# Fetching the experts' weights and tokens one step ahead, and issuing sinkhorn's steps in smaller pieces

## The chip, the cores and the metric

The kernel runs on one core of one Trainium2 chip. A core has TensorE (PE, with its weight loads as PEld), VectorE (DVE), ScalarE (ACT), GpSimd (POOL) and SyncE (SP), which here only issues DMAs. Each engine works through its own instructions in the order in which they were issued. The metric is the device time of one execution in microseconds, as the median of several runs.

## The reference, cut to what matters

```python
# 1. delta-rule attention, 768 steps for 4 x 8 heads; its output is x, 3072 x 384
# 2. a dense layer: h = x @ w_in (384 x 2048); x = (h * tanh(softplus(h))) @ w_out
# 3. eight experts, mixed by a doubly normalised gate
logits = x @ w_gate                       # 3072 x 8
P = np.exp(logits - logits.max())
for _ in range(8):
    P /= P.sum(1, keepdims=True) + 1e-09
    P /= P.sum(0, keepdims=True) + 1e-09
    P *= N / E
for e in range(E):
    h = np.maximum(x @ w1[e], 0.0)        # 384 x 1024
    out += P[:, e:e + 1] * (h @ w2[e])    # 1024 x 384
```

## The kernel before

The tokens are cut into six blocks of 512 (NBLK). The **first part** goes through the blocks one by one: attention, the dense layer in 16 steps (s0 to s15, with f1 to f4 behind them), and expert 0 in 8 steps (s16 to s23). Every step uses one weight tile `w` of 768 KB out of six slots; `conversions` asks for the next tile at the end of a step (L242, `w<-wd`). Each block's x goes to DRAM as `x2d`, expert 0's sum as `y0d`.

The **second part** does experts 1 to 7 in 168 *pairs* `(e, i, g)`: expert, block, and one of four groups of 256 hidden columns; g runs fastest, then i. For pair p, `first(p)` (L470) makes the seven sums of a fast block-matrix scheme (33 matmuls) in four PSUM banks b0 to b3. Two of them come from pool `ps_h`, two from `ps_a`; both pools have two buffers. `evacuate(p)` adds them up on DVE (L493 to L496), with a copy and a relu on ACT (L492, L497), and splits the result into a high and a low part `gh`, `gl` (L498). `second(p)` (L1329) multiplies them by w2 into the banks `o`. PE's order is first(p), second(p-1), first(p+1) and so on.

Around this the following is issued in program order, so that each piece stands in a place of its own on each engine:

- `g_load` brings one group's weights: two DMAs into the one raw tile `gr` (L401, L405, issued by `g_fetch` within g_load), four additions on DVE (L421 to L424), two copies on ACT (L426), four subtractions on POOL (L428). Five slots (`gslots`) hold results; two of them lie in memory that comes free only when the first part is over. Loads 0 to 2 stand at s1, s5 and s9 of the last block, loads 3 and 4 ahead of first(0), the others behind the second products of an expert's last block.
- `x_begin(i)` fetches a block's tokens into the one raw tile `gxr` (L436) and makes four sums on DVE (L438 to L441); `x_split` splits them in three portions on ACT and POOL (L448, L449); `x_store` writes the result to DRAM as `xcd` (2304 KB), from where later experts read it by `x_load` (L457). In expert 1 block i+1 is begun at g = 0, split at g = 1 to 3 and stored at g = 3, where `acc_load(i + 2)` also fetches an accumulator from `y0d` (L1350).
- The sinkhorn normalisation is a list `sinks`, of which `sink_step` takes one. `sink_start` has two small products on PE, `sink_round` is DVE alone (L349 to L353), `sink_round_end` begins with a product on PE of what the round left (L357, 8 columns, in a `ps_a` buffer) and goes on on DVE (L359 to L362). Two steps are taken per step s17 to s23 of the last block, then two per pair.
- When the list is empty, each pair scales two quarters of an accumulator by expert 0's gate on DVE (L1390).

Of the kernel before, what the change touches and what calls it, by code (L numbers as in the profile page):

```python
# [28 lines left out]
U1 = DFF // 128  # L29
# [55 lines left out]
def delta_mish_sinkhorn_kernel(  # L85
# [245 lines left out]

    def sink_start():
        m1, m2, m3 = sk["m"][:, 0:1], sk["m"][0:1, 1:2], sk["m"][:, 2:3]
        nc.vector.tensor_reduce(out=m1, in_=Pf, axis=AX.X, op=ALU.max)
        ps = small[0]()
        nc.tensor.transpose(ps[0:1, 0:128], m1, id_sb)
        nc.vector.tensor_reduce(out=m2, in_=ps[0:1, 0:128], axis=AX.X, op=ALU.max, negate=True)
        ps2 = small[0]()[:, 0:1]
        mm(ps2, lhsT=sk["ones"][0:1, :], rhs=m2, start=True, stop=True)
        nc.vector.tensor_copy(m3, ps2)  # L340
        nc.scalar.activation(out=Pf, in_=Pf, func=AF.Sigmoid, bias=m3)
        d = sk["d"]
        nc.vector.tensor_scalar(out=d, in0=Pf, scalar1=-1.0, scalar2=1.0, op0=ALU.mult, op1=ALU.add)
        nc.vector.reciprocal(out=d, in_=d)
        nc.vector.tensor_tensor(out=Pf, in0=Pf, in1=d, op=ALU.mult)
# [18 lines left out]
    sinks = deque([sink_start, lambda: None] + [sink_round, sink_round_end] * ROUNDS)  # L364
# [32 lines left out]
    def g_fetch(n):  # L397
# [11 lines left out]
        return r  # L409

    def g_load():
# [6 lines left out]
        r = g_fetch(n)  # L418
# [6 lines left out]
        for at in (1024, 0):  # L425
            nc.scalar.activation(out=w[:, 0, at:at + 1024], in_=r[:, at:at + 1024], func=AF.Copy)  # L426
            for q in (at, at + 512):
                nc.gpsimd.tensor_tensor(  # L428
                    out=w[:, 1, q:q + 512], in0=r[:, q:q + 512], in1=w[:, 0, q:q + 512].bitcast(F32), op=ALU.subtract
                )  # L430

    def x_begin(i):

        c = order[i]
        r = pool2["xr"].tile([128, NX, 256], F32, tag="xr", name="gxr")
        nc.sync.dma_start(out=r[:, 0:6].rearrange("p a x -> p (a x)"), in_=x2_dram[c].rearrange("p k x -> p (k x)"))  # L436
# [5 lines left out]
        xraw[i] = r  # L442
# [67 lines left out]
    if True:  # L510
# [708 lines left out]
        with tc.manual_schedule():  # L1219
            banks[:] = [0, [A1, A1]]  # L1220
            for c in range(NBLK):
                pe, rest, late = window(c)
                if c == NBLK - 1:
                    p1.close()
                    open_second()
                    for f, step in ((1, g_load), (5, g_load), (9, g_load)):
                        rest[f"s{f}"].append(step)
                    rest["s12"].append(lambda: x_begin(0))
                    for k in range(3):
                        rest[f"s{13 + k}"].append(lambda k=k: x_split(0, k))  # L1230
                    rest["f1"].append(lambda: x_store(0))
# [49 lines left out]
                for f in range(U1, NU):  # L1281
# [9 lines left out]
                    if c == NBLK - 1 and f > U1:  # L1291
                        sink_step()
                    if f > U1 + 1:
                        y0_second(u - 2)
                    if c == NBLK - 1 and f > U1:
                        sink_step()
# [46 lines left out]
    with tc.manual_schedule():  # L1343
# [12 lines left out]
        while gnext[0] < NGS:  # L1356
            g_load()
        for p in range(N + 1):
# [6 lines left out]
            if p >= 1:  # L1365
                second(p - 1)
                if pairs[p - 1][1] == NBLK - 1:
                    g_load()
            if p < N:
                if e == 1:  # L1370
                    if i + 1 < NBLK:
                        if g == 0:
                            x_begin(i + 1)
                        elif g < NGR - 1:
                            x_split(i + 1, g - 1)
                        else:
                            x_split(i + 1, 2)
                            x_store(i + 1)
                            acc_load(i + 2)
                    elif g == NGR - 1:  # L1380
                        x_load(p + 1)
                elif g == 1 and p + NGR < N:
                    x_load(p - 1 + NGR)
# [70 lines left out]
```

## Time and profile before

| | |
|---|---|
| median of 3 runs | 2407.23 us (2403.13 to 2412.72) |
| the profiled execution, its own time | 2409.84 us |
| its span, first to last instruction | 2408.1 us |
| mean granted TensorE clock | 0.960 of full speed |
| PE busy | 2260.9 us, 94% |
| PEld, DVE, ACT, POOL busy | 2092.1, 1228.7, 619.7, 529.0 us |

A timeline row gives the start (us from the span's start), the length, the engine, the line, the operation, what it writes and reads, how many instructions were merged, and in square brackets the idle time of its engine just before it with what ended that. An idle time of PE is what the end can move by; an idle time of DVE, ACT or POOL counts only where PE waits for them. The last block's first part begins near 836 us, the second part at 951.20 us.

### The profile page before, as it was taken

What the parts mean: (1) busy time and instruction counts of PE and PEld (TensorE: products, weight loads), DVE (VectorE), ACT (ScalarE), POOL (GpSimd) and SP (SyncE); (2) the same over time, 40 slices, a digit from 0 to 9 for tenths busy, and PEclk for the clock granted to TensorE, in tenths of its full rate; (3) what the DMA queues carried; (4) which work ended last, traced back from release to release, by engine and by line L of the source; (5) the groups of instructions that cost most, each with busy time, mean ns of one, the idle gap of its engine ahead of it and who ended that gap; (6) DMA issues with size and microseconds to landing.
All of it is one profiled execution on the core that took longest, in us unless ns stands there. A gap on an engine that the chain in (4) does not pass through costs nothing.

```text
span 2408.1 us, 41970 instructions
## 1 busy us (share of the span) xinstructions
PE 2260.9 (94%) x18012; PEld 2092.1 (87%) x18012; DVE 1228.7 (51%) x2009; ACT 619.7 (26%) x1012; POOL 529.0 (22%) x439
## 2 busy tenths in 40 slices
PE   6698899999999998598989999999999999999998
PEld 3477788788887877598989999999999999999998
DVE  8874726426171204554545455555555555555554
ACT  4244331333322241212221121122122113112111
POOL 5586441332412060211210030020011003002000
PEclk7799999999999999799989999999999999999999
DMA  5357634536344474133132221222212223212321
GB/s 170 115 203 220 221 133 149 185 132 223 130 169 155 163 246 182 41 117 132 69 142 79 93 88 71 93 93 105 89 56 105 79 93 119 79 72 88 105 78 55
DMA packets 74442, 297.05 MB, mean 123 GB/s; under 512 B 7504, under 2 KB 39504, under 8 KB 68880
## 3 DMA queue, kind: packets, MB, share of 16 engines
q1 hardware_dynamic: 74256, 294.36, 35.3%
q8 instruction: 142, 2.33, 0.4%
q14 instruction: 44, 0.36, 0.0%
HBM read 247.15 MB, written 47.19 MB: 122 GB/s over the span
## 4 chain that ended last, share of the span: by engine, by line
PE 33%; issue 11%; DMA 6%; POOL 3%; SPq 0%; ACT 0%; DVE 0%; POOLq 0%; DVEq 0%; ACTq 0%
PE b L470 17%; PE o L1329 16%; DMA gr<-in_w_dram 5%; POOL gw L428 2%; POOL gx L428 1%; DMA acc<-y0d 1%; DMA gx<-xcd 0%; SPq L401 0%; DVE gt L493 0%; ACT gw L426 0%; POOL gx L449 0%; DVE acc L1334 0%; ACT gh L497 0%; SPq L457 0%; ACT gx L448 0%
## 5 line engine op out<-in xcount | busy, mean ns | idle before, releaser
L470 PE MATMUL b<-gx,gw 128*128 128x256 f32 x3564 | 457.4, 286 | 11.0 <-DVE gt L493 6.3
L470 PEld LDWEIGHTS b<-gx,gw 128*128 128x128 f32 x3564 | 449.4, 195 | 15.5 <-DVE gt L493 7.8
L1329 PE MATMUL o<-gw,gh 128*128 128x384 f32 x1728 | 440.9, 336 | 2.3 <-DVE acc L1334 2.3
L497 ACT ACTIVATE gh<-gt 128x1024 fp32r<-128x1024 f32 x168 | 178.3, 1062 | 657.0 <-DVE gt L496 657.0
L1329 PEld LDWEIGHTS o<-gw,gh 128*128 128x128 f32 x1728 | 307.7, 189 | 3.0 <-issue 2.1
L296 PE MATMUL psh<-xh,w 128*128 128x512 f32 x864 | 290.3, 418 | 19.1 <-DMA w<-wd 6.8
L498 DVE SCALAR_TENSOR_TENSOR gl<-gt,gh 128x1024 fp32r<-128x1024 f32 x168 | 207.3, 1234 | 189.5 <-ACT gh L497 189.5
L1329 PE MATMUL o<-gw,gl 128*128 128x384 f32 x864 | 289.7, 335 | 0.0
L493 DVE TENSOR_TENSOR gt<-b,gt 128x512 f32<-128x512 f32 x168 | 116.1, 691 | 316.5 <-PE b L470 257.1
L470 PE MATMUL b<-gx,gx 128*128 128x256 f32 x1980 | 246.1, 282 | 13.5 <-DMA gx<-xcd 12.5
L470 PEld LDWEIGHTS b<-gx,gx 128*128 128x128 f32 x1980 | 242.7, 190 | 15.2 <-issue 13.2
L1329 PE MATMUL o<-gx,gh 128*128 128x384 f32 x960 | 247.5, 339 | 1.6 <-DVE acc L1334 1.6
L428 POOL TENSOR_TENSOR gw<-gr,gw 128x512 fp32r<-128x512 f32 x72 | 90.7, 1294 | 573.4 <-ACT gw L426 573.4
L296 PEld LDWEIGHTS psh<-xh,w 128*128 128x128 f32 x864 | 161.2, 196 | 60.0 <-issue 12.3
L961 POOL TENSOR_TENSOR gl<-x,gh 128x512 fp32r<-128x512 f32 x96 | 128.6, 1341 | 381.7 <-ACT gh L960 381.5
L296 PE MATMUL psh<-xl,w 128*128 128x512 f32 x432 | 176.2, 408 | 4.2 <-DVE xl L590 4.2
L1329 PEld LDWEIGHTS o<-gx,gh 128*128 128x128 f32 x960 | 171.6, 188 | 1.9 <-issue 1.0
L1329 PEld LDWEIGHTS o<-gw,gl 128*128 128x128 f32 x864 | 162.6, 188 | 0.3 <-DVE gl L498 0.2
L1329 PE MATMUL o<-gx,gl 128*128 128x384 f32 x480 | 162.7, 339 | 0.0
L492 ACT ACTIVATE gt<-b 128x256 f32<-128x256 f32 x168 | 64.2, 382 | 370.6 <-PE b L470 347.9
L972 PE MATMUL x<-gh,w 128*128 128x512 f32 x576 | 149.5, 395 | 0.0
L428 POOL TENSOR_TENSOR gx<-gr,gx 128x512 fp32r<-128x512 f32 x40 | 50.3, 1290 | 430.7 <-ACT gx L426 430.7
(182 smaller groups left out, 2993.0 us busy)
## 6 DMA issues: line engine op xcount, KB each, us to landing
w<-wd SPq DMA_DIRECT2D x120, 768.0 KB, 4.5
gx<-xcd SPq DMA_DIRECT2D x36, 2304.0 KB, 8.9
gr<-in_w_dram SPq DMA_DIRECT2D x56, 384.0 KB, 3.7
wd<-w SPq DMA_DIRECT2D x24, 768.0 KB, 4.6
xcd<-gx SPq DMA_DIRECT2D x6, 2304.0 KB, 7.9
kq<-in_qkb_dram SPq DMA_DIRECT2D x20, 256.0 KB, 7.0
vt<-in_vtok_dram SPq DMA_DIRECT2D x6, 768.0 KB, 8.4
kq<-in_w_in_dram SPq DMA_DIRECT2D x12, 384.0 KB, 4.6
```

What stands on the lines that cost most here:

```text
L296: mm(ps, lhsT=wi(u, pw, kc), rhs=(xh, xl)[px][:, kc, :], start=(n == 0), stop=(n == 3 * KD - 1))
L428: nc.gpsimd.tensor_tensor(out=w[:, 1, q:q + 512], in0=r[:, q:q + 512], in1=w[:, 0, q:q + 512].bitcast(F32), op=ALU.subtract)
L470: mm(ps, lhsT=w[:, pw, a * 128:a * 128 + 128], rhs=x[:, px, b, :], start=(n == 0), stop=(n == last))
L492: nc.scalar.activation(out=t[:, 7], in_=b0[:, 0], func=AF.Copy)
L493: tt(out=t[:, 0:7:6], in0=b1, in1=t[:, 7:8].to_broadcast([128, 2, 256]), op=ALU.add)
L497: nc.scalar.activation(out=h, in_=t[:, 0:4], func=AF.Relu)
L498: nc.vector.scalar_tensor_tensor(out=l, in0=t[:, 0:4], scalar=0.0, in1=h.bitcast(F32), op0=ALU.max, op1=ALU.subtract)
L961: nc.gpsimd.tensor_tensor(out=l, in0=p, in1=h.bitcast(F32), op=ALU.subtract)
L972: mm(x2ps[c][k], lhsT=wo(u, pw, k * 128, k * 128 + 128), rhs=(h, l)[pg], start=(f == 0 and n == 0), stop=(f == U1 - 1 and n == 2))
L1329: mm(o[t], lhsT=(h, l)[ph][:, z, (t % 2) * 128:(t % 2) * 128 + 128], rhs=w[:, pw, at:at + DM], start=(g == 0 and fi == 0 and n == 0), stop ...
```

## The change

- `g_fetch` leaves `g_load` and stands at its end, for the next load. The very first one is issued alone at s1; g_loads 0 to 2 move to s5, s9 and s13.
- `x_fetch` leaves `x_begin`. Block 0 is fetched at s1, block 1 at s15, block i + 2 when block i + 1 has been split, ahead of that block's store and the accumulator. x_begin(0) and its splits move to s7, s8, s10 and s11, its store to s15.
- g_loads 3 and 4 no longer stand ahead of first(0) but behind second(0) and second(4) (`p in (1, 5)`). The following loads stay where they were.
- `x_load` is issued at g = 0 instead of g = 1 (four pairs ahead instead of three); the first one, for expert 2, is issued at pair 20 instead of pair 23.
- `sink_start` is divided into sink_max, sink_max_all and sink_start with empty steps between them. The list has 22 entries instead of 18. In s17 to s23 two steps are taken together, ahead of expert 0's second product. In the pairs two are taken behind evacuate(p) and two more behind second(p-1).

```diff
@@ -329,12 +329,16 @@
     P = lg
     Pf = lg.rearrange("p t e -> p (t e)")
 
+    def sink_max():
+        nc.vector.tensor_reduce(out=sk["m"][:, 0:1], in_=Pf, axis=AX.X, op=ALU.max)
+
+    def sink_max_all():
+        ps = small[0]()
+        nc.tensor.transpose(ps[0:1, 0:128], sk["m"][:, 0:1], id_sb)
+        nc.vector.tensor_reduce(out=sk["m"][0:1, 1:2], in_=ps[0:1, 0:128], axis=AX.X, op=ALU.max, negate=True)
+
     def sink_start():
-        m1, m2, m3 = sk["m"][:, 0:1], sk["m"][0:1, 1:2], sk["m"][:, 2:3]
-        nc.vector.tensor_reduce(out=m1, in_=Pf, axis=AX.X, op=ALU.max)
-        ps = small[0]()
-        nc.tensor.transpose(ps[0:1, 0:128], m1, id_sb)
-        nc.vector.tensor_reduce(out=m2, in_=ps[0:1, 0:128], axis=AX.X, op=ALU.max, negate=True)
+        m2, m3 = sk["m"][0:1, 1:2], sk["m"][:, 2:3]
         ps2 = small[0]()[:, 0:1]
         mm(ps2, lhsT=sk["ones"][0:1, :], rhs=m2, start=True, stop=True)
         nc.vector.tensor_copy(m3, ps2)
@@ -361,7 +365,9 @@
         nc.vector.tensor_scalar(out=cr, in0=cr, scalar1=float(NTOK) / E, scalar2=None, op0=ALU.mult)
         nc.vector.tensor_tensor(out=P, in0=P, in1=cr[:, None, :].to_broadcast([128, NT, E]), op=ALU.mult)
 
-    sinks = deque([sink_start, lambda: None] + [sink_round, sink_round_end] * ROUNDS)
+
+    none = lambda: None
+    sinks = deque([sink_max, none, sink_max_all, none, sink_start] + [sink_round, sink_round_end] * ROUNDS + [none])
 
     def sink_step():
         if sinks:
@@ -394,7 +400,12 @@
         pool2["t"] = ctx.enter_context(tc.tile_pool(name="gt", bufs=1))
         pool2["h"] = ctx.enter_context(tc.tile_pool(name="gh", bufs=2))
 
-    def g_fetch(n):
+    graws = []
+
+    def g_fetch():
+        n = len(graws)
+        if n >= len(gloads):
+            return
         e, g = gloads[n]
         f0 = g * 256
         r = pool2["r"].tile([128, GW], F32, tag="r", name="gr")
@@ -406,7 +417,7 @@
             out=r[:, 10 * 128:].rearrange("p (a d) -> p a d", a=2),
             in_=w2[e, f0:f0 + 256, :].rearrange("(a p) d -> p a d", p=128),
         )
-        return r
+        graws.append(r)
 
     def g_load():
 
@@ -415,7 +426,7 @@
             return
         gnext[0] += 1
         w = gslots[n % NGS]
-        r = g_fetch(n)
+        r = graws[n]
         v = r[:, 0:10 * 128].rearrange("p (a x) -> p a x", x=128)
         tt = nc.vector.tensor_tensor
         tt(out=v[:, 6], in0=v[:, 1], in1=v[:, 3], op=ALU.add)
@@ -428,18 +439,24 @@
                 nc.gpsimd.tensor_tensor(
                     out=w[:, 1, q:q + 512], in0=r[:, q:q + 512], in1=w[:, 0, q:q + 512].bitcast(F32), op=ALU.subtract
                 )
-
-    def x_begin(i):
-
+        g_fetch()
+
+    def x_fetch(i):
+        if i >= NBLK:
+            return
         c = order[i]
         r = pool2["xr"].tile([128, NX, 256], F32, tag="xr", name="gxr")
         nc.sync.dma_start(out=r[:, 0:6].rearrange("p a x -> p (a x)"), in_=x2_dram[c].rearrange("p k x -> p (k x)"))
+        xraw[i] = r
+
+    def x_begin(i):
+
+        r = xraw[i]
         tt = nc.vector.tensor_tensor
         tt(out=r[:, 6], in0=r[:, 1], in1=r[:, 0], op=ALU.subtract)
         tt(out=r[:, 8], in0=r[:, 3], in1=r[:, 1], op=ALU.subtract)
         tt(out=r[:, 7], in0=r[:, 3], in1=r[:, 6], op=ALU.subtract)
         tt(out=r[:, 1], in0=r[:, 2], in1=r[:, 7], op=ALU.subtract)
-        xraw[i] = r
         xq[i] = pool2["x"].tile([128, 2, NX, 256], F32R, tag="x", name="gx")
 
     def x_split(i, k):
@@ -1223,12 +1240,15 @@
                 if c == NBLK - 1:
                     p1.close()
                     open_second()
-                    for f, step in ((1, g_load), (5, g_load), (9, g_load)):
-                        rest[f"s{f}"].append(step)
-                    rest["s12"].append(lambda: x_begin(0))
-                    for k in range(3):
-                        rest[f"s{13 + k}"].append(lambda k=k: x_split(0, k))
-                    rest["f1"].append(lambda: x_store(0))
+                    rest["s1"].append(g_fetch)
+                    rest["s1"].append(lambda: x_fetch(0))
+                    for f in (5, 9, 13):
+                        rest[f"s{f}"].append(g_load)
+                    rest["s7"].append(lambda: x_begin(0))
+                    for k, f in enumerate((8, 10, 11)):
+                        rest[f"s{f}"].append(lambda k=k: x_split(0, k))
+                    rest["s15"].append(lambda: x_store(0))
+                    rest["s15"].append(lambda: x_fetch(1))
                 m0 = PLACES[0][0]
                 b = c * NU
 
@@ -1290,10 +1310,9 @@
                         fill(3.6 if c == 0 else 3.2)
                     if c == NBLK - 1 and f > U1:
                         sink_step()
+                        sink_step()
                     if f > U1 + 1:
                         y0_second(u - 2)
-                    if c == NBLK - 1 and f > U1:
-                        sink_step()
                     conversions(u)
                 e_relu(b + NU - 1)
                 split = [lambda kc=kc: st_x1(c + 1, kc) for kc in range(KD)] if c + 1 < NBLK else []
@@ -1353,8 +1372,6 @@
 
         acc_load(0)
         acc_load(1)
-        while gnext[0] < NGS:
-            g_load()
         for p in range(N + 1):
             if p < N:
                 e, i, g = pairs[p]
@@ -1364,23 +1381,23 @@
                 sink_step()
             if p >= 1:
                 second(p - 1)
-                if pairs[p - 1][1] == NBLK - 1:
+                sink_step()
+                sink_step()
+                if pairs[p - 1][1] == NBLK - 1 or p in (1, 5):
                     g_load()
             if p < N:
-                if e == 1:
-                    if i + 1 < NBLK:
-                        if g == 0:
-                            x_begin(i + 1)
-                        elif g < NGR - 1:
-                            x_split(i + 1, g - 1)
-                        else:
-                            x_split(i + 1, 2)
-                            x_store(i + 1)
-                            acc_load(i + 2)
-                    elif g == NGR - 1:
-                        x_load(p + 1)
-                elif g == 1 and p + NGR < N:
-                    x_load(p - 1 + NGR)
+                if e == 1 and i + 1 < NBLK:
+                    if g == 0:
+                        x_begin(i + 1)
+                    elif g < NGR - 1:
+                        x_split(i + 1, g - 1)
+                    else:
+                        x_split(i + 1, 2)
+                        x_fetch(i + 2)
+                        x_store(i + 1)
+                        acc_load(i + 2)
+                elif g == 0 and p + NGR < N:
+                    x_load(p + NGR)
             if not sinks and todo:
                 for _ in range(2):
                     if not todo or order.index(todo[0][0]) >= have[0]:
```

How the order of DVE moves, behind the last copy of expert 0's sum. `gr` is the raw weight tile, `b` the banks of pair 0, `gate` and `lg` belong to sinkhorn. Before:

```order
L421 TENSOR_TENSOR gr<-gr 128x128
L422 TENSOR_TENSOR gr<-gr 128x256
L423 TENSOR_TENSOR gr<-gr 128x128
L424 TENSOR_TENSOR gr<-gr 128x128
L493 TENSOR_TENSOR gt<-b_8691,gt 128x2x256
L494 TENSOR_TENSOR gt<-b_8701,gt 128x512
L495 TENSOR_TENSOR gt<-b_8701,gt 128x256
L496 TENSOR_TENSOR gt<-b_8711,gt 128x512
L498 SCALAR_TENSOR_TENSOR gl<-gt,gh 128x1024
L349 TENSOR_REDUCE gate<-lg 128x24
```

and now:

```order
L607 COPY xr<-y_8394 128x384
L510 TENSOR_TENSOR gt<-b_8653,gt 128x2x256
L511 TENSOR_TENSOR gt<-b_8663,gt 128x512
L512 TENSOR_TENSOR gt<-b_8663,gt 128x256
L513 TENSOR_TENSOR gt<-b_8673,gt 128x512
L515 SCALAR_TENSOR_TENSOR gl<-gt,gh 128x1024
L363 TENSOR_SCALAR gate<-psa 128x8
L364 RECIPROCAL gate<-gate 128x8
L365 TENSOR_SCALAR gate<-gate 128x8
L366 TENSOR_TENSOR lg<-lg,gate 128x192
L353 TENSOR_REDUCE gate<-lg 128x24
```

The weight sums of load 4 (those of load 3 stand ahead of them in the same way) are gone from the front of pair 0's sums, and the pair is followed by the end of a sinkhorn round instead of the beginning of one.

The order of PE between the second products of pairs 0 and 1 (`gw_7827` to `gw_7829` are the slots of groups 0 to 2, `psa` is a sinkhorn product). Before:

```order
L1329 MATMUL o_8813<-gw_7827,gh 128x384 x2
L1329 MATMUL o_8813<-gw_7827,gl 128x384
L470 MATMUL b_8842<-gx,gw_7829 128x256 x3
L470 MATMUL b_8846<-gx,gw_7829 128x256 x9
L470 MATMUL b_8856<-gx,gw_7829 128x256 x9
L470 MATMUL b_8866<-gx,gw_7829 128x256 x12
L1329 MATMUL o_8810<-gw_7828,gh 128x384 x2
```

and now:

```order
L1348 MATMUL o_8773<-gw_7827,gh 128x384 x2
L1348 MATMUL o_8773<-gw_7827,gl 128x384
L361 MATMUL psa<-gate 128x8
L487 MATMUL b_8824<-gx,gw_7829 128x256 x3
L487 MATMUL b_8828<-gx,gw_7829 128x256 x9
L487 MATMUL b_8838<-gx,gw_7829 128x256 x9
L487 MATMUL b_8848<-gx,gw_7829 128x256 x12
L361 MATMUL psa<-gate 128x8
L1348 MATMUL o_8770<-gw_7828,gh 128x384 x2
```

Sinkhorn's products, of which two stood in pairs 0 and 1 (one each, behind the first products), are now four: one behind first(0), one behind first(1), and the two seen here.

The order of SP where expert 1 prepares a block (`x2d` is read, `xcd` written, `acc` an accumulator). Before:

```order
L436 DMA gxr<-x2d_81 128x1536
L452 DMA xcd_117<-gx 128x4608
L1350 DMA acc_8652<-y0d_76 128x1536
L436 DMA gxr<-x2d_82 128x1536
L452 DMA xcd_118<-gx 128x4608
```

and now:

```order
L449 DMA gxr<-x2d_82 128x1536
L469 DMA xcd_117<-gx 128x4608
L1369 DMA acc_8640<-y0d_76 128x1536
L449 DMA gxr<-x2d_83 128x1536
L469 DMA xcd_118<-gx 128x4608
L1369 DMA acc_8641<-y0d_77 128x1536
```

The read of the next block's tokens has moved from behind the accumulator to ahead of the store.

## Rows read from the trace of the kernel before

**Rows 1.** Who PE waited for, from 840 us on: us in total, times, longest

```profile
PE psa L357 <- DVE gate L353: 35.9, 3, 28.9
PE b L470 <- DMA gx<-xcd: 12.5, 1, 12.5
```

**Rows 2.** Timeline of PE, 846 to 1020 us: start, length, what, idle before

```profile
850.61 1.15 PE L296 MATMUL psh<-xh,w 128*128 128x512 f32 x2 [3.73 <-ACT x L954]
...
951.20 4.11 PE L470 MATMUL b<-gx,gw 128*128 128x256 f32 x33
984.24 0.57 PE L357 MATMUL psa<-gate 128*128 128x8 f32 x2 [28.93 <-DVE gate L353]
...
1003.62 4.11 PE L470 MATMUL b<-gx,gw 128*128 128x256 f32 x33
...
1011.74 4.04 PE L470 MATMUL b<-gx,gx 128*128 128x256 f32 x33
```

**Rows 3.** Timeline of PE, 1019 to 1439 us: first products of six pairs

```profile
1019.78 4.45 PE L470 MATMUL b<-gx,gw 128*128 128x256 f32 x33
...
1104.93 5.59 PE L470 MATMUL b<-gx,gw 128*128 128x256 f32 x30 [2.92 <-DVE gt L493]
...
1213.93 6.56 PE L470 MATMUL b<-gx,gx 128*128 128x256 f32 x33 [12.52 <-DMA gx<-xcd]
...
1249.00 4.04 PE L470 MATMUL b<-gx,gx 128*128 128x256 f32 x33
...
1411.33 4.04 PE L470 MATMUL b<-gx,gx 128*128 128x256 f32 x33
...
1438.14 4.11 PE L470 MATMUL b<-gx,gw 128*128 128x256 f32 x33
```

**Rows 4.** Timelines of DVE, ACT and POOL ahead of pair 0's sums

```profile
963.20 0.29 DVE L421 TENSOR_TENSOR gr<-gr 128x128 f32<-128x128 f32 x1 [11.24 <-DMA gr<-in_w_dram]
...
973.78 0.29 DVE L421 TENSOR_TENSOR gr<-gr 128x128 f32<-128x128 f32 x1 [9.43 <-DMA gr<-in_w_dram]
...
964.44 2.00 ACT L426 ACTIVATE gx<-gr 128x1024 fp32r<-128x1024 f32 x2 [13.08 <-DVE gr L424]
...
965.63 4.93 POOL L428 TENSOR_TENSOR gx<-gr,gx 128x512 fp32r<-128x512 f32 x4 [58.60 <-ACT gx L426]
```

**Rows 5.** Two stretches: length, busy by engine (PE to POOL), granted clock, DMA share, GB/s

```profile
850.61:854.36 3.75, 3.75 (x10) 2.94 (x10) 0.00 (x0) 1.72 (x3) 3.75 (x4) 0.54 0.57 233
1104.93:1110.52 5.59, 5.58 (x31) 5.40 (x32) 4.38 (x7) 1.44 (x2) 0.00 (x0) 0.69 0.00 0
```

**Rows 6.** Timeline of SP's queue: four weight tiles asked for in the last block

```profile
860.72 12.56 SPq L242 DMA_DIRECT2D w<-wd  x4
```

**Rows 7.** DMA issues by what they move: count, KB each, median us to landing

```profile
w<-wd SPq DMA_DIRECT2D x120, 768.0 KB, 4.5
...
acc<-y0d SPq DMA_DIRECT2D x6, 768.0 KB, 9.4
```

**Rows 8.** Timeline of DVE: first and last sum of pair 2

```profile
1005.32 0.69 DVE L493 TENSOR_TENSOR gt<-b,gt 128x512 f32<-128x512 f32 x1 [5.26 <-PE b L470]
...
1009.59 1.23 DVE L498 SCALAR_TENSOR_TENSOR gl<-gt,gh 128x1024 fp32r<-128x1024 f32 x1 [1.13 <-ACT gh L497]
```

**Rows 9.** Timeline of DVE: the end of one sinkhorn round and the next round

```profile
929.56 0.17 DVE L359 TENSOR_SCALAR gate<-psa 128x8 f32<-128x8 f32 x1 [1.06 <-PE psa L357]
...
930.20 0.36 DVE L362 TENSOR_TENSOR lg<-lg,gate 128x192 f32<-128x192 f32 x1
...
931.08 0.34 DVE L349 TENSOR_REDUCE gate<-lg 128x24 f32<-128x192 f32 x1
...
932.40 0.52 DVE L353 TENSOR_REDUCE gate<-lg 128x8 f32<-128x192 f32 x1
```

**Rows 10.** Timeline of DVE: its waits for tokens and for an accumulator in expert 1

```profile
1033.71 0.43 DVE L438 TENSOR_TENSOR gxr<-gxr 128x256 f32<-128x256 f32 x1 [4.29 <-DMA gxr<-x2d]
...
1103.53 0.75 DVE L1390 TENSOR_SCALAR acc<-acc,lg 128x384 f32<-128x384 f32 x2 [11.48 <-DMA acc<-y0d]
```

## The prediction

> **What bounds the kernel now.** I read the overview first: PE is busy for 94% of the span, so only PE's idle time, and work done at the lower of its two clock levels, can be won. Then I asked whom PE waited for in the part that the change touches. Two entries stand out [rows 1]: sinkhorn's 8-column product L357 waits 35.9 us for DVE, nearly all of it in two places, and the first products wait 12.5 us for `gx`, a block's tokens. The timeline of PE gives the places [rows 2, 3]: 3.73 us in step s3 of the last block; 28.93 us between first(0) and first(1); 2.92 us in pair 13; 12.52 us ahead of pair 24. In the undisturbed stretch a pair takes (1411.33 - 1249.00)/20 = 8.12 us [rows 3], 4.1 of them for first [rows 2] and so 4.0 for second; there nothing can be won.
>
> The timelines of the other engines say why [rows 4]. Ahead of pair 0's sums DVE, ACT and POOL work through loads 3 and 4, and DVE waits 11.24 and 9.43 us for their raw tiles, each asked for only then. Pair 0's sums stand behind that, sinkhorn's round behind the sums, and PE's next product behind the round.
>
> I take the change in three stretches; e5 to e8 are the ends of sinkhorn's rounds 5 to 8, r6 to r8 the rounds.
>
> **Last block of the first part.** Removed: at s1 ACT waited with load 0's copies for a raw tile just asked for, and the dense layer's own copy stood behind it. That is the 3.73 us [rows 2]; the matmuls behind it ran for 3.75 us at a granted clock of 0.54 [rows 5], nearly the lower level of 1.2 GHz instead of 2.4, so 3.75 x 0.46 = 1.7 us are lost there. 5.4 us won. Now the first load's work begins at s5 with its tile landed.
>
> Added: g_fetch at the end of g_load waits, on SP's queue, until POOL has freed the raw tile, and the weight tiles of the following steps are queued behind it. They are asked for one per (12.56 - 0.32)/3 = 4.08 us [rows 6], three steps = 12.2 us ahead of need; a landing takes 4.5 us [rows 7], so the queue may be held for 7.7 us. From the step's start the hold is about 0.2 us until ACT is free, half its 2.00 us of copies, 0.5 us of another POOL operation and POOL's 4.93 [rows 4]: 6.6 us. Then come g_fetch's own two issues (some 0.9 us) and its 768 KB ahead of the tile's. 2304 + 768 KB took 9.4 us [rows 7], so 768 KB are at most 2.3 us, of which the issues cover 0.9. The tile is late by 6.6 + 0.9 + 1.4 - 7.7 = 1.2 us, at s8 and at s12; at s16 the layer's end gives slack. x_fetch(0) at s1 puts another 2.3 us ahead of a tile: about 1 us at s4. So 3.4 us lost; bounds 0 (all inside slack) and 9 (three times 3). Sinkhorn's steps in s17 to s23 have at least 3 us per step on DVE and PE for two of them; I cost that at nothing, as the one wait of 0.8 us there (35.9 - 28.9 - 6.2 in the row of the waits) is replaced by one of like size. **Net +2 us** (-4 to +5).
>
> **Pairs 0 to 2.** Before, first(3) begins 1011.74 - 951.20 = 60.5 us after first(0) [rows 2]. The new chain, in us from first(0): pair 0's sums begin at 1.7 and end at 7.2, as pair 2's did after first(2) [rows 2, 8]. PE's product e5 waits for nothing late; r5 ended in the first part. DVE goes on with e5 (929.56 to 930.56, 1.0 us) and r6 (931.08 to 932.92, 1.84 us) [rows 9] to 10.0, then x_begin(1), four sums of 0.43 us [rows 10], to 11.7. Here is the new wait: PE has ended first(1) near 8.7, and e6's product needs r6 and a `ps_a` buffer that pair 1's first sum frees, at 11.7 + 0.7 = 12.4. PE idles 3.7 us. Pair 1's sums take up to 5.5 us [rows 8], to 17.2; e6 and r7 to 20.0. PE has done second(0) by 16.7 (by 18.6 at the lower clock) and idles again until e7 at 20.2. DVE: e7 to 21.7, r8 to 23.5; then load 3's sums, ACT's copies from 24.7 (1.24 us behind the sums' start, as 964.44 to 963.20) to 26.7 [rows 4], a split's copy to 27.6, pair 2's copy and first sum to 28.7, which frees the buffer for e8. PE, done with first(2) at 24.6, idles 4.1 us. second(1) follows, and first(3) begins at 33. Load 3's slot is ready at 24.7 + 1.2 + 4.93 = 30.8, under that cover; without it every us more of POOL would count. After 2.92 us of idling 30 matmuls took 5.59 us where 33 take 4.11 [rows 3], 1.85 us more, at a granted clock of 0.69 [rows 5]; one such loss falls into PE's own time: 34.5, rounded. **Gain 60.5 - 34.5 = 26 us.** Bounds: three pairs' PE work alone is 20.3, with the first idling 24, a gain of 36; with three clock losses and DVE's order worse by 2 us in each pair 42, a gain of 18.
>
> **Pairs 3 to 25.** Before, pairs 3 to 23 took 1213.93 - 1011.74 = 202.2 us instead of 21 x 8.12 = 170.5: 31.7 us lost, and 6.56 - 4.04 = 2.5 us more at the lower clock in pair 24 [rows 2, 3], 34.2 in all. The 12.52 us go: pair 24's tokens are now asked for four pairs ahead and in front of the fetches that wait for POOL. The wait of 4.29 us for tokens [rows 10], which made later splits late, goes too. What stays or comes:
> - the last split of a block comes 0.4 us late in pairs 4, 12, 16 and 20 (4.45 for 4.04) [rows 3]: 1.6 us. In pair 8, behind load 4's work in pair 5, I put 2 us.
> - accumulators 4 and 5 are still scaled right behind their fetch; DVE waits 11.48 us [rows 10] and PE stops in pairs 13 and 17: 2.92 + 1.85 = 4.8 us each. The x_fetch is now ahead of store and accumulator on the queue: 2.3 us later. 2 x 7.1 = 14.2 us. The wait for accumulator 3 goes, as the list ends a pair later and its scaling falls into pair 8.
> - at the change to expert 2 there is now no slack from a wait, so it costs what the change to expert 3 does: three pairs in 1438.14 - 1411.33 = 26.8 us instead of 24.3 [rows 3], 2.5 us.
>
> Together 20.3 us instead of 34.2: **gain 14 us** (bounds 5 and 20). The later changes of expert stay: their four raw tiles are fetched when POOL frees the one buffer, before and after.
>
> The page "DMA: Bandwidth & Descriptors" of the Trainium skill (section on queues, rings and completion order) says that an engine takes the descriptors of one ring in their order, which here speaks against the change, since the accumulator is queued behind one more transfer. By its fit of 2 us and 436 GB/s (section on the anatomy of one DMA, given there for the other way of issuing) 3.9 MB would land 11 us after the issue, an estimate, where I have 9.4 + 2.3 = 11.7; the two stops would be 0.7 us shorter and the sum 1.4 us better. The median of 9.4 us for 3.1 MB agrees with that fit (9.2 us).
>
> **Sum.** 2 + 26 + 14 = 42 us. The profiled execution took 2409.84 us, 2.6 above the median of the runs; so 2368 for it, and **2365 us** for the median.
>
> **Rivals.**
> 1. *Smoother than that.* The queue's holds stay within slack, the accumulators land no later, second(1) hides the idling: 3.4 + 4.6 + 8 us more, 2349 us. For it: each of these is a small excess over a slack. Against: DVE's chain e6, r7, e7, r8 has no slack.
> 2. *DVE's chain costs more.* If first(3) begins at 42 and pair 8 loses 8 us as its late split did before, 7.5 + 6 us less, and with three tiles late by 3 us 5 more: 2384 us. For it: the four places where PE waits for DVE are now close together.
> 3. *The waits only move.* Load 3 stands in front of pair 2's sums as loads 3 and 4 stood in front of pair 0's; if its raw tile were not there in time, the 26 us would be lost again, and if pair 24's tokens collided with the weights, 12 more: 42 - 38 = 4 us are left, 2403 us. Against: the tile is asked for at s13, 40 us earlier.
> 4. *Slower: SP's queue.* Each g_fetch that waits for POOL holds the weight tiles behind it, at s5, s9 and s13. Beyond 7.7 us each us costs PE one; the point from which the whole gain and the bound of no change are spent is a hold of 7.7 + (42 + 12)/3 = 26 us. At 28 us it is 61 - 42 = 19 us slower, 2426 us. DVE, ACT and POOL once took over 20 us for two loads [rows 4], but waiting for DMAs that are now done before; so unlikely.
>
> **How the numbers follow.** The forecast has 0.61, rival 1 0.16, rival 2 0.14, rival 3 0.05, rival 4 0.04. The range takes the forecast with rivals 1 and nearly all of 2, 2348 to 2383 us. A measurement of this kernel can tell some 0.5%, 12 us, from no change: faster is forecast and rivals 1 and 2 (0.91), the same rival 3 (0.05), slower rival 4 (0.04).
>
> **What would show it.** PE's 28.93, 12.52 and 3.73 us gone; three idlings of 3 to 4 us around L361 in pairs 1 and 2; first(3) some 34 us behind first(0); waits for DVE in pairs 13 and 17 of about 5 us; `w` tiles named in waits at s8 and s12; 8.12 us per pair afterwards. I am wrong if PE waits over 6 us for L361 or if a `w` tile stops PE for over 3 us, and in the other direction if first(3) comes within 28 us.

## The result, and the profile after

The changed kernel takes **2371.1 us** (median of 4 runs, 2370.12 to 2376.89), the kernel before on the same chip 2405.35; the ratio is 0.9857 (95%: 0.983 to 0.9885), 34 us less. The profiled execution took 2370.12 us with a span of 2368.3, that of before 2409.84 with 2408.1.

The 39.8 us between those two spans are not all the change's: block 4's logits, before which nothing was changed, come 5.8 us earlier in the new profile. So the stretches are counted from there (all in us, each from the start of the first of PE's products named to that of the next; a last row for the whole; first(28) stands four pairs behind the change to expert 2):

| from ... to | before | after | gain | forecast |
|---|---|---|---|---|
| logits of block 4 to first(0) | 146.1 | 150.8 | -4.8 | +2 |
| first(0) to first(3) | 60.5 | 33.1 | 27.4 | 26 |
| first(3) to first(28) | 237.3 | 225.0 | 12.2 | 14 |
| first(28) to the end | 1159.1 | 1160.0 | -0.9 | 0 |
| logits of block 4 to the end | 1602.9 | 1569.0 | 33.9 | 42 |

Whom PE waited for from 840 us on, after (us in total, times, longest):

```profile
PE b L487 <- DVE gt L510: 12.4, 2, 6.6
PE psa L361 <- DVE gt L510: 6.3, 2, 3.2
PE psh L296 <- DMA w<-wd: 6.1, 4, 2.3
...
PE b L487 <- POOL gx L466: 2.1, 2, 1.5
PE psa L361 <- DVE gate L357: 0.3, 1, 0.3
```

Both entries of [rows 1] are gone: no wait for `gx`, and of sinkhorn's 35.9 us 6.6 are left. In their place stand weight tiles, which were no entry of the list before, and a longer wait of the first products for DVE, which before was

```profile
PE b L470 <- DVE gt L493: 6.3, 3, 3.0
```

PE's timeline gives the places (start, length, what, idle before), to be held against [rows 2, 3]:

```profile
864.85 0.70 PE L296 MATMUL psh<-xh,w 128*128 128x512 f32 x2 [2.31 <-DMA w<-wd]
885.40 0.70 PE L296 MATMUL psh<-xh,w 128*128 128x512 f32 x2 [2.32 <-DMA w<-wd]
...
950.19 4.11 PE L487 MATMUL b<-gx,gw 128*128 128x256 f32 x33
...
962.27 0.60 PE L361 MATMUL psa<-gate 128*128 128x8 f32 x2 [3.06 <-DVE gt L510]
969.84 4.20 PE L487 MATMUL b<-gx,gw 128*128 128x256 f32 x33
977.26 0.39 PE L361 MATMUL psa<-gate 128*128 128x8 f32 x2 [3.23 <-DVE gt L510]
983.33 4.04 PE L487 MATMUL b<-gx,gx 128*128 128x256 f32 x33
```
```profile
1026.37 3.61 PE L487 MATMUL b<-gx,gw 128*128 128x256 f32 x28 [1.45 <-POOL gx L466]
...
1074.53 5.32 PE L487 MATMUL b<-gx,gw 128*128 128x256 f32 x30 [6.60 <-DVE gt L510]
...
1114.85 5.59 PE L487 MATMUL b<-gx,gw 128*128 128x256 f32 x30 [5.81 <-DVE gt L510]
```

The 28.93 us have become 3.06 and 3.23; the 12.52 us ahead of pair 24 are gone, and so are the 3.73 us of s3; in their place stand 2.31 and 2.32 at s8 and s12, which the forecast had at 1.2 each. SP's queue shows why (start, length, what, count):

```profile
856.81 0.38 SPq L412 DMA_DIRECT2D gr<-in_w_dram  x1
857.25 0.48 SPq L416 DMA_DIRECT2D gr<-in_w_dram  x1
857.77 5.12 SPq L242 DMA_DIRECT2D w<-wd  x4
```

Nothing is issued from 845.5 to 856.81, while the fetch at the end of load 0 waits for POOL to free `gr`; then four weight tiles go out in 5.12 us that were due over 12.56 [rows 6]. The first of them lands 6.9 us after its issue, where 4.5 + 1.4 was put, and PE goes on at 864.85. POOL's row gives the end of the wait, and a row of windows the matmuls behind the stop at a mean granted clock of 0.67, between the two levels of 1.2 and 2.4 GHz (columns as in [rows 5]):

```profile
851.74 5.05 POOL L439 TENSOR_TENSOR gw<-gr,gw 128x512 fp32r<-128x512 f32 x4
```
```profile
864.85:870.00 5.15, 5.15 (x16) 4.08 (x17) 0.00 (x0) 0.60 (x1) 0.92 (x1) 0.67 0.76 316
```

### The profile page after: what moved, and what is told of

Read it like the earlier page. It is cut to its first block, busy times and chain, and to the rows that moved or that the text cites. A ratio compares the mean times of both kernels' runs of the same rounds, so it can differ in the third digit from the quotient of the medians.

```text
span 2368.3 us, 41965 instructions
## 1 busy us (share of the span) xinstructions
PE 2254.5 (95%) x18012; PEld 2084.9 (88%) x18012; DVE 1236.1 (52%) x2009; ACT 619.7 (26%) x1012; POOL 529.4 (22%) x439
## 3 DMA queue, kind: packets, MB, share of 16 engines
q8 instruction: 142, 2.33, 0.4%
## 4 chain that ended last, share of the span: by engine, by line
issue 35%; PE 10%; DMA 5%; POOL 4%; DVE 1%; SPq 0%; ACT 0%; POOLq 0%; DVEq 0%; ACTq 0%
PE o L1348 5%; PE b L487 5%; DMA gr<-in_w_dram 4%; POOL gw L439 2%; POOL gx L439 1%; DMA acc<-y0d 1%; SPq L412 0%; POOL gx L466 0%; DVE acc L1353 0%; ACT gh L514 0%; DVE gt L510 0%; DVE gt L513 0%; ACT gw L437 0%; DVE gt L511 0%; DVE acc L1407 0%
## 5 line engine op out<-in xcount | busy, mean ns | idle before, releaser
L487 PE MATMUL b<-gx,gw 128*128 128x256 f32 x3564 | 452.5, 284 | 17.7 <-DVE gt L510 12.4
L487 PEld LDWEIGHTS b<-gx,gw 128*128 128x128 f32 x3564 | 444.2, 192 | 22.5 <-DVE gt L510 14.1
```

Source lines behind the costliest of these rows:

```text
L487: mm(ps, lhsT=w[:, pw, a * 128:a * 128 + 128], rhs=x[:, px, b, :], start=(n == 0), stop=(n == last))
```

## The experiments

My theory: loads 3 and 4 moved off pair 0 won the 27 us, tokens fetched early the 12, and the losses that are left are each a queue in which work stands behind something that waits. The main rival for the first: sinkhorn's division won it. Stretches of all kernels (their profiled executions; the first column is where block 4's logits begin):

| kernel | median us | logits 4 | to first(0) | to first(3) | to first(28) | to the end | from logits 4 |
|---|---|---|---|---|---|---|---|
| before | 2405.4 | 805.1 | 146.1 | 60.5 | 237.3 | 1159.1 | 1602.9 |
| after | 2371.1 | 799.3 | 150.8 | 33.1 | 225.0 | 1160.0 | 1569.0 |
| after, again | 2374.0 | 804.0 | 146.3 | 33.9 | 226.9 | 1160.2 | 1567.3 |
| e1 | 2364.6 | 805.4 | 140.2 | 34.1 | 224.7 | 1158.7 | 1557.7 |
| e2 | 2381.7 | 805.8 | 147.9 | 35.4 | 233.5 | 1159.8 | 1576.7 |
| e3 | 2397.2 | 803.2 | 143.2 | 52.8 | 234.7 | 1160.6 | 1591.3 |
| e4 | 2397.8 | 811.5 | 150.9 | 33.9 | 249.9 | 1160.6 | 1595.4 |
| e5 | 2352.0 | 801.6 | 146.2 | 33.9 | 208.1 | 1159.4 | 1547.6 |
| e6 | 2370.5 | 799.3 | 147.6 | 23.6 | 234.3 | 1159.2 | 1564.9 |
| e6b | 2368.3 | 797.5 | 149.1 | 31.4 | 226.8 | 1160.0 | 1567.3 |
| e7 | 2354.1 | 795.1 | 146.7 | 32.8 | 224.8 | 1148.0 | 1552.3 |
| e8 | 2330.2 | 799.0 | 139.2 | 31.4 | 204.8 | 1147.9 | 1523.3 |
| e9 | 2320.9 | 799.9 | 139.2 | 21.8 | 205.7 | 1147.9 | 1514.6 |

**The change once more.**

> The changed kernel once more, for the scatter between executions. Theory A (the first five blocks of the first part, which the change leaves alone, differ by some us from one execution to the next): the logits of block 4 come between 795 and 811 us after the start, and from there to the end it takes 1569 us within 3 us. Theory B (the part behind scatters as much): that stretch differs by more than 5 us.

2373.96 us; logits of block 4 at 804.0 and 1567.3 us from there: theory A. Over all thirteen profiles the untouched part ends between 795.1 and 811.5 us, more than most single edits are worth, so what follows is read by stretches. "To first(0)" scatters too: the six executions whose code there is that of the change (after twice, e4, e5, e6, e7) have 146.2 to 150.9, in the mean 148.1. What scatters there is the clock and not the waiting. This is the stretch in the changed kernel and in its second execution (columns as in [rows 5]):

```profile
799.34:950.19 150.85, 144.23 (x679) 122.55 (x677) 40.59 (x90) 44.30 (x70) 40.99 (x31) 0.95 0.57 211
```
```profile
804.01:950.28 146.27, 139.53 (x678) 119.28 (x677) 40.26 (x90) 44.27 (x70) 41.11 (x31) 0.99 0.59 218
```

PE idles 6.6 and 6.7 us, nearly the same; its busy time differs by 4.7 us, at a granted clock of 0.95 and 0.99. Over the six the idle time is 6.3 to 7.0 us and the busy time 139.5 to 144.3. Nor is the lower clock tied to the length of a stop: behind the 2.31 us above it was 0.67, behind a stop of 2.23 us at s12 of the second execution it was 1.00:

```profile
887.85:893.00 5.15, 5.15 (x23) 4.24 (x24) 0.03 (x1) 1.96 (x3) 0.60 (x1) 1.00 0.83 347
```

Why it fell behind one and not behind the other is not shown. So in this stretch a difference of less than some 5 us between two single executions says nothing by itself.

**e1: the fetch two steps later.**

```diff
-                    for f in (5, 9, 13):
-                        rest[f"s{f}"].append(g_load)
+                    for f, m in ((5, "s7"), (9, "s11"), (13, "f2")):
+                        rest[f"s{f}"].append(lambda: g_load(False))
+                        rest[m].append(g_fetch)
```

(`g_load(False)` leaves out its g_fetch.)

> The fetch of the next raw tile stands two steps behind each load in the last block (s7, s11, f2), when POOL has long freed the buffer; the bytes are the same. Theory A (the issue that waits for POOL holds the weight tiles queued behind it): PE's stops for w of 2.31 and 2.32 us at s8 and s12 go, and so do the some 2 us of slower matmuls behind each; from the logits of block 4 to those of block 5 some 103 us instead of 111.1, the whole run 8 us below the changed kernel. Theory B (the 768 KB ahead of the tile make it late, wherever they stand): two stops of about 2 us stay, at s10 and s14, 111 us, no gain.

2364.63 us, ratio to before 0.9823 (0.98 to 0.9847). Logits to logits took 104.2 us (107.2 to 112.0 in the six executions with the change's code), and to first(0) 140.2 instead of 148.1 in the mean: 8 us, as theory A has it. The idle time falls from 6.6 us in the mean to 1.4; the other 2.6 us are busy time, which goes with the clock. The stretch, PE's waits from 840 to 950 us, and SP's queue:

```profile
805.41:945.65 140.24, 138.87 (x678) 119.89 (x677) 39.61 (x90) 44.30 (x70) 41.16 (x31) 0.99 0.63 227
```
```profile
PE psh L296 <- DMA w<-wd: 0.8, 1, 0.8
PE psa L361 <- DVE gate L357: 0.3, 1, 0.3
```
```profile
845.71 16.69 SPq L242 DMA_DIRECT2D w<-wd  x6
864.48 0.38 SPq L412 DMA_DIRECT2D gr<-in_w_dram  x1
```

Six tiles now go out one after the other, and the raw tile's fetch waits for nothing. Only the 0.8 us at s4 stays. The same bytes cost nothing from another place in the queue: it was the waiting issue that cost.

**e2: sinkhorn as before, in the changed kernel.**

```diff
-    sinks = deque([sink_max, none, sink_max_all, none, sink_start] + [sink_round, sink_round_end] * ROUNDS + [none])
+    sinks = deque([sink_start, none] + [sink_round, sink_round_end] * ROUNDS)
...
                 second(p - 1)
-                sink_step()
-                sink_step()
```

> The changed kernel with sinkhorn as before: 18 undivided steps, at their old places, two behind the sums of pairs 0 and 1. Theory A (moving loads 3 and 4 won pairs 0 to 2, the division little): first(3) some 38 us behind first(0) instead of 33.1, two idlings of about 5 us at L357's counterpart in pairs 0 and 1; 5 us slower than the changed kernel. Theory B (the division won them): first(3) 50 us or more behind first(0), 17 us or more slower. In the last block no difference over 1 us by either.

2381.67 us, ratio to before 0.9891 (0.9869 to 0.9912). first(3) came 35.4 us after first(0), with the two idlings of 5 us, so with the loads moved the division is worth 2 us in these pairs, and the rest of the change wins the others. From the logits on e2 is 7.7 us behind the change, and most of that stands elsewhere. PE's timeline (a kernel's lines move by a few with its edit):

```profile
962.75 0.51 PE L363 MATMUL psa<-gate 128*128 128x8 f32 x2 [4.96 <-DVE gate L359]
...
973.62 0.57 PE L363 MATMUL psa<-gate 128*128 128x8 f32 x2 [4.96 <-DVE gate L359]
...
1046.94 5.88 PE L489 MATMUL b<-gx,gw 128*128 128x256 f32 x30 [6.58 <-DVE gt L512]
```

The old list ends a pair earlier, so accumulator 3 is scaled a pair earlier, and DVE waits for it, ahead of the sums that hold PE in pair 9 (6.58); the prediction's "the wait for accumulator 3 goes, as the list ends a pair later" is this stop.

**e3: the new sinkhorn alone, in the kernel before.** The reverse of e2's edit.

> The kernel before with sinkhorn divided and placed as in the change, and nothing else. Theory A: loads 3 and 4 still stand ahead of pair 0's sums on DVE, and PE's next product behind them: the wait of 28.9 us shrinks to some 21 us, since e5 needs only a freed buffer and not a round of its own, first(3) some 50 to 57 us behind first(0), a gain of 4 to 10 us over the kernel before. Theory B (the division is what counts): first(3) some 35 us behind first(0), a gain of 25 us.

2397.22 us, ratio to before 0.9959 (0.9946 to 0.9973). first(3) at 52.8 us, and one stop, as theory A has it:

```profile
973.25 0.60 PE L361 MATMUL psa<-gate 128*128 128x8 f32 x2 [22.72 <-DVE gt L498]
```

By stretches the division alone wins 11.6 us, 7.7 of them between first(0) and first(3). The rest of the change without it (e2) wins 26.2, and both together 33.9: a little less than the sum. Ahead of first(0) e3 is 2.8 us shorter than the kernel before, but this does not show a gain of the division there (before, then e3):

```profile
805.15:951.20 146.05, 140.94 (x683) 121.28 (x681) 38.64 (x103) 44.03 (x70) 40.93 (x31) 0.98 0.59 207
```
```profile
803.20:946.42 143.22, 138.94 (x678) 119.81 (x677) 35.78 (x90) 44.17 (x70) 40.89 (x31) 0.99 0.59 211
```

PE's idle time falls by 0.8 us only, the other 2.0 are busy time at another clock, within the scatter above; and e2, which has the old sinkhorn, took 147.9 there against the mean of 148.1.

Not separated: e2 and e3 split off sinkhorn, but that loads 3 and 4 stand behind pair 0's sums and that their raw tiles are asked for a step ahead were only run together. What either is worth alone is open.

**e4: tokens asked for at their old places.**

```diff
                 elif g == 0 and p + NGR < N:
-                    x_load(p + NGR)
+                elif e == 1 and g == NGR - 1:
+                    x_load(p + 1)
+                elif e > 1 and g == 1 and p + NGR < N:
+                    x_load(p - 1 + NGR)
```

> The changed kernel with the tokens of experts 2 to 7 asked for at their old places (behind the last pair of expert 1, and from then on three pairs ahead), nothing else. Theory A: PE waits some 12 us for gx ahead of pair 24, as before, and the three pairs of the change to expert 2 lose none of their 2.5 us on top; 10 to 12.5 us slower than the changed kernel, nothing else differs. Theory B (the fetch collides with the raw tiles in either order, or something else hides it): a wait under 4 us.

2397.8 us, ratio to before 0.9965 (0.9951 to 0.998), some 26 us above the change. Both theories miss: A named the right wait, at half its size. PE's timeline and SP's queue:

```profile
1211.03 6.71 PE L487 MATMUL b<-gx,gx 128*128 128x256 f32 x33 [21.90 <-DMA gx<-xcd]
```
```profile
1199.85 0.37 SPq L412 DMA_DIRECT2D gr<-in_w_dram  x1
1200.26 0.49 SPq L416 DMA_DIRECT2D gr<-in_w_dram  x1
1200.86 0.40 SPq L474 DMA_DIRECT2D gx<-xcd  x1
```

PE had been idle since 1189.13; the tokens went out at 1200.86, behind the third fetch that had waited for POOL. With the fetches at the end of each load, a place behind them costs 9 us more than it did before. Tokens ahead of the fetches were thus worth more than the 12.5 us of [rows 1].

**e5: accumulators scaled two pairs later.**

```diff
-                have[0] = i + 1
...
+                if e == 1 and g == 1:
+                    have[0] = max(have[0], i + 2)
```

(`have` starts at 2.)

> The changed kernel with accumulators 2 to 5 scaled two pairs later (from the second pair of the next block on); their fetch is asked for at the same place. Theory A (DVE stands in its queue waiting for the accumulator, and the sums behind it hold PE): the stops of 6.60 and 5.81 us in pairs 13 and 17 go, with the 1.85 us of slower matmuls behind each; both pairs about 8.5 us instead of 16.4 and 15.9, 15 us below the changed kernel. Theory B (the split of the block's tokens, late for another reason, holds PE there): stops of 3 us or more stay, a gain under 8 us.

2352.04 us, ratio to before 0.9783 (0.9763 to 0.9802). first(3) to first(28) takes 208.1 us instead of 225.0 and 226.9: 17 to 19 us, theory A. Neither stop is left. In the changed kernel DVE's row shows the wait (two tiles of accumulator 4):

```profile
1073.12 0.75 DVE L1407 TENSOR_SCALAR acc<-acc,lg 128x384 f32<-128x384 f32 x2 [15.15 <-DMA acc<-y0d]
```

**e6: sinkhorn's steps behind the second products only.**

```diff
                 evacuate(p)
-                sink_step()
-                sink_step()
+                if p == 0:
+                    sink_step()
+                    sink_step()
...
-                for _ in range(2):
+                for _ in range(4 if p == 3 else 2):
```

> The changed kernel with sinkhorn's steps two per pair behind the second products alone from pair 1 on (in pair 0 behind the sums, as now), so that the list ends in pair 3, where block 0's four tiles are then scaled at once. Theory A (a product behind the sums of its own pair waits for a buffer those sums free): of the stops of 3.06 and 3.23 us at L361 none is left over 1 us, first(3) 28 us or less behind first(0) instead of 33.1, 5 us or more won. Theory B (it is DVE's chain of sums, steps and x_begin that is late, whatever PE does meanwhile; PE then stops in first(2) for a buffer instead): a stop of 2 to 4 us comes in first(2), first(3) 30 to 33 us behind first(0), under 3 us won.

2370.48 us, ratio to before 0.9862 (0.984 to 0.9885): no difference to the change. first(3) came after 23.6 us, better than theory A, and yet first(5) 48.2 us after first(0), where the change has 49.7. PE's timeline tells where the 9.5 us went:

```profile
970.31 0.39 PE L361 MATMUL psa<-gate 128*128 128x8 f32 x2 [1.15 <-DVE gt L510]
...
971.52 6.09 PE L487 MATMUL b<-gx,gx 128*128 128x256 f32 x32 [0.60 <-POOL gx L439]
...
983.89 0.50 PE L487 MATMUL b<-gx,gw 128*128 128x256 f32 x2 [1.54 <-ACT gx L465]
986.07 4.20 PE L487 MATMUL b<-gx,gw 128*128 128x256 f32 x22 [1.68 <-POOL gx L466]
```

PE arrives earlier at first(3) and first(4) and there meets load 3 and block 1's split tokens, which had been done under sinkhorn's waits: the cover that the prediction named for load 3. From first(3) to first(5) e6 takes 24.5 us where the change takes 16.6; 3.8 of the 8 us more are the last three stops above, the rest are slower matmuls behind them, at a granted clock of 0.71 from 971.52 to 977.44 and of 0.65 from 986.07 to 990.30.

**e6b: x_begin(1) in s20.**

```diff
+                    rest["s20"].append(lambda: x_begin(1))
...
                     if g == 0:
-                        x_begin(i + 1)
+                        if i:
+                            x_begin(i + 1)
```

> The changed kernel with x_begin(1), the four sums of block 1's tokens, moved from pair 0 to s20 of the last block. Theory A (the four sums of 0.43 us stand ahead of pair 1's sums on DVE, as the prediction has it): the stop of 3.06 us shrinks by 1.7 us to some 1.4 us, the second one of 3.23 us by no more than 1.7; 2 to 4 us below the changed kernel. Theory B (the steps of sinkhorn alone set it): 3.06 and 3.23 stay within 0.3 us.

2368.27 us, ratio to before 0.9849 (0.9831 to 0.9868); the stop of 3.06 became 1.60, the one of 3.23 stayed, and first(0) to first(3) fell by 2 us: theory A at its lower end. The four sums did stand ahead of pair 1's sums.

**e7: the loads at a change of expert spread.**

```diff
-                if pairs[p - 1][1] == NBLK - 1 or p in (1, 5):
+                if p in (1, 5) or p > NBLK * NGR - NGR and p % (NBLK * NGR) in (21, 23, 1, 4):
```

> The changed kernel with the four loads at a change of expert behind pairs 20, 22, 24 and 27 (of each 24) instead of 20, 21, 22 and 23. Theory A (loads in four pairs running pile work on ACT and DVE, and the first pairs of the next expert come late): the two pairs of 9.8 and 8.9 us at each of the six changes fall to 8.1 to 8.5, 10 to 15 us below the changed kernel. Theory B (the cost belongs to the change itself, new weights and the accumulators' sums, wherever the loads stand): 9.8 and 8.9 us stay within 0.3 us, no gain.

2354.07 us, ratio to before 0.9788 (0.9766 to 0.981). From first(28) on 1148.0 us instead of 1160.0, and at the changes every pair lies within 0.25 us of 8.12: theory A. ACT's row at the second load of a change, first in the changed kernel, then in e7:

```profile
1167.91 2.01 ACT L437 ACTIVATE gw<-gr 128x1024 fp32r<-128x1024 f32 x2 [4.52 <-DMA gr<-in_w_dram]
```
```profile
1166.52 2.01 ACT L437 ACTIVATE gw<-gr 128x1024 fp32r<-128x1024 f32 x2 [1.83 <-DVE gr L433]
```

With one raw buffer a load's fetch, copies and subtractions follow one another, one load in 10.5 us (the changed kernel's next two copies start at 1178.51 and 1189.01), and a pair has 8.12. Four pairs running cannot hold four loads, and ACT, in order, takes the next pair's copy only behind them.

**e8: these together** (e1, e5, e6b, e7, and load 4 behind pair 15: `p in (1, 16)`).

> The changed kernel with the later fetches of e1, the later scaling of e5, x_begin(1) at s20 of e6b and the spread loads of e7, and load 4 behind pair 15 instead of pair 4. Theory A (these are separate losses, each on PE's path): from the logits of block 4 to the end 11 + 17 + 2 + 12 us less than the changed kernel's 1569 us, and 2 us for the stop of 1.45 us ahead of pair 8: 1525 us; the median 40 to 45 us below the changed kernel, 2326 to 2331 us. Theory B (one loss hides behind another, an engine other than PE becomes the bound): under 30 us of the 44.

2330.2 us, ratio to before 0.9683 (0.9657 to 0.9708); 1523.3 us from the logits on: theory A to 2 us. The losses were separate.

**e9: e8 with e6 and its two obstacles moved.**

```diff
+                    for k in range(3):
+                        rest[f"s{21 + k}"].append(lambda k=k: x_split(1, k))
...
+                if p == 1:
+                    g_load()
```

(Block 1's later splits and load 3's old place fall away.)

> The kernel of e8 with sinkhorn's steps behind the second products (as in e6), block 1's tokens split in s21 to s23 of the last block, and load 3 right behind pair 1's sums. Theory A (in e6 PE stopped for load 3 and for block 1's tokens in place of sinkhorn's products, so with these out of the way the gain stays): first(4) some 33 us behind first(0), no single stop over 1.5 us there, 5 to 8 us below e8. Theory B (DVE's chain of sums, steps and scaling sets these pairs whatever stands beside it): first(4) 38 us or more behind first(0), within 3 us of e8.

**2320.86 us**, ratio to before 0.9637 (0.961 to 0.9663): the fastest here. first(4) came 30.7 us after first(0), and 9 us were won over e8, a little more than theory A. All that PE still waits for from 840 us on:

```profile
PE psh L296 <- DMA w<-wd: 0.8, 1, 0.8
PE b L488 <- POOL gx L467: 0.7, 2, 0.4
PE psa L361 <- DVE gate L357: 0.5, 2, 0.3
PE psh L296 <- ACT xh L996: 0.2, 1, 0.2
PE b L488 <- DVE gt L514: 0.2, 1, 0.2
```

## Why the prediction was right, and where it was off

2365 us were forecast and 2371.1 measured, inside the range, faster as forecast; 42 us of gain became 34.

- **Pairs 0 to 2** (26 forecast, 27.4 measured). The chain was right: PE stops of 3.06 and 3.23 us behind sums and steps, where 3.7 and 4.1 were put. The idling between them, put at up to 3.5 us, is absent in this profile and 0.9 us in the second execution: second(0) took 7.0 us instead of 4.0, at a granted clock of 0.58, and so ended when DVE was ready. e2 and e3 show that most of the gain here is not sinkhorn's, and e6b that x_begin stands in that chain.
- **Pairs 3 to 25** (14 forecast, 12.2 measured). Pair 24's tokens, the 2 us of pair 8 and the 2.5 us at the change to expert 2 came as put. The two stops for accumulators cost 8.3 and 7.8 us over a pair of 8.12, where 7.1 each was put. The accumulators landed 12.6 and 11.8 us after their issue, where I had 11.7 (rows below the list). The fit of 2 us and 436 GB/s in the Trainium skill, page "DMA: Bandwidth & Descriptors" (section "Anatomy of one DMA", for the other way of issuing), gives 11 us, an estimate; counted from the first of the three issues the trace has 13.4 and 12.6, so it is short in both. e5 shows that the stops were DVE's place in its queue: both go when the scaling is taken two pairs later.
- **Last block of the first part** (a gain of 2 forecast, a loss of 4.8 measured in the profile, 2.1 in the mean of six executions against the one of before). This is the step that failed: "The tile is late by 6.6 + 0.9 + 1.4 - 7.7 = 1.2 us, at s8 and at s12; at s16 the layer's end gives slack." The hold was as long as put: POOL was done 6.7 us after the step began, near 850.1. But the tile took 6.9 us to land instead of 4.5 + 1.4, and a tile was late by 0.65 us behind the logits as well, where slack was put. In all PE stopped for `w` for 6.1 us (5.7 to 6.5 in the six) instead of 3.4. The clock is the other half: 1.7 us were put as won behind the stop that goes and nothing as lost behind those that come, and the busy time of the stretch rose instead, from 140.9 us to 141.5 in the mean of the six. e1, which takes the hold away, leaves 0.8 us of the stops and gives 8 us back where 2.4 were put. That the division would change nothing here was put, and no run shows otherwise.
- **Signs.** `w` tiles at s8 and s12, two of the three idlings around L361 and stops of 5.8 and 6.6 us in pairs 13 and 17 came. Neither sign of being wrong did: the longest single wait for L361 was 3.23 us, for a `w` tile 2.32. The 6 us for L361 have to be read as one wait; all of them together are 6.6, where the forecast's first and last alone were 7.8.
- **Rivals.** Rival 4 named the mechanism; the hold was a quarter of the 26 us from which it would have decided, and so it made the gain smaller and not negative. Rival 1's smoother course did not come by itself: it took e1 for the queue and e5 for the accumulators.

The two accumulators (KB, us from issue to landing):

```profile
acc<-y0d SPq DMA_DIRECT2D x1, 768.0 KB, 12.6
```
```profile
acc<-y0d SPq DMA_DIRECT2D x1, 768.0 KB, 11.8
```

Left open: why the tile behind the raw tile lands so late. From the raw tile's first issue at 856.81 to that tile's landing 7.9 us later this was moved:

```profile
DMA packets 934, 2.27 MB, mean 288 GB/s; under 512 B 52, under 2 KB 692, under 8 KB 934
```

The raw tile and the tile itself are 1.57 MB. No other transfer than the later tiles was in flight, so some 0.7 MB of those were moved before the first one was complete. Whether it would have come in time without them was not tried; in e1 a tile issued at 866.16 behind a raw tile, with another tile still landing ahead of it and none issued behind it for 4 us, landed 5.8 us later, 7.5 us after the raw tile's first issue at 864.48. So the 0.9 + 1.4 + 4.5 = 6.8 us that were put for this were too few there as well.

## What to carry to other kernels

An asynchronous fetch is only as asynchronous as the queue that issues it: place it where its buffer is already free, or it holds everything behind it, and price the catch-up along with the hold, and the clock, which fell behind some of the stops here and not behind others. The same goes for a compute engine in order: work that waits for a transfer belongs where the transfer has landed, not where it was asked for. And when a wait is removed, look for what it had covered: e6 won 9.5 us by first(3) and had 1.5 left by first(5), until two covered pieces were moved as well (e9).

## What the runs showed of the hardware that was not expected

The DMA engines stand still while SP's issue waits, from 851 to 857.5 us in the changed kernel, and then move up to 442 GB/s. From 850 to 870 us in 40 slices of 0.5 us (busy tenths, then GB/s):

```profile
DMA  9300000000000000699978989899999999998410
GB/s 430 123 0 0 0 0 0 0 0 0 0 0 0 0 0 29 152 354 369 313 273 304 344 344 356 332 418 369 393 418 430 418 418 430 442 406 344 168 49 25
```

Scaling two tiles on DVE took 0.75 us when POOL stood still (1073.12 above) and 2.33 us in e5, where POOL subtracts from 1047.30 to 1049.46:

```profile
1047.67 2.33 DVE L1408 TENSOR_SCALAR acc<-acc,lg 128x384 f32<-128x384 f32 x2
```
```profile
1047.30 2.16 POOL L466 TENSOR_TENSOR gx<-gxr,gx 128x768 fp32r<-128x768 f32 x1 [5.79 <-ACT gx L465]
```

The Trainium skill, "SBUF — State Buffer" (section "Who interferes with whom"), says that such a DVE operation can take the port pair that DVE and GpSimd share, and that whichever comes second is then blocked. The rows agree: DVE starts behind POOL and ends 0.5 us after it, 1.6 us later than alone. e5 is faster all the same.
